# A block retention and two dense stages on one core: forming the scaled queries on GpSimd, and converting the second piece of the first weights inside the retention

## The chip, the cores and the metric

The kernel runs on one core of a Trainium2 chip. The metric is the device time of one execution in microseconds. Three runs of the kernel before gave 575.89, 576.50 and 577.19 us, a median of 576.5 us. The engines are called PE (matrix multiply), DVE (VectorE), ACT (ScalarE), POOL (GpSimd) and SP (the queue that issues most DMAs).

## The reference, cut to what matters

```python
for b in range(nb):                       # blocks along the sequence, per batch and head
    intra = (qb @ kb.T) * Dmask           # Dmask[i, j] = lam ** (i - j) for i >= j
    intra = intra @ vb
    inter = (qb * lam_pow) @ kv_state     # lam_pow[i] = lam ** (i + 1)
    out[block] = intra + inter
    kv_state = lam_block * kv_state + (kb * rev_pow).T @ vb
x = out as (1536, 512)                    # tokens by heads * head_dim
x = relu(x @ w_in) ** 2 @ w_out           # first dense stage, weights (512, 2048) and (2048, 512)
x = leaky(x @ w_in2) @ w_out2             # second dense stage, slope 0.01
```

Batch is 2, heads 8, sequence 768, head dimension 64. The weights arrive as 64-bit floats.

## The kernel before, in words

The retention is computed in chunks of 128 positions: 2 batches of 6 chunks give 12 units, called u0 to u11 here. A unit needs k, q and v (three loads of 256 KB, line 201). Of k and q PE makes transposes (L294), which ACT copies out of PSUM as kT and qT (L298). PE then forms raw scores (L311); DVE multiplies them by the table of powers and so makes Pm (mask, L316, two instructions of 128x512). Queries scaled by their powers, qS, are made by DVE out of the PSUM bank of the transposes (scale_q, L304); the first unit of a batch (u0, u6) needs none. The state of a unit is a product of v and decayed keys kd (PE L335; kd is made by POOL, L329), to which DVE adds the old state times a power (tmp by POOL at L342, sum st by DVE at L347, two instructions; L349 at the start of a batch). The output of a unit takes qS with the state of the unit before (L360) and Pm with v (L362). It leaves PSUM as a high part (ACT, L68, xhi) and a low part (DVE, L69, xlo), because each later product is made of three products of high and low parts.

PE's and SP's order in the retention is the program's own order. One pass of the loop at L391, called i, does: transposes and scaled queries of unit i+2, loads of k and q of unit i+4 and of v of unit i+2, at some i a fetch of a raw piece of weights, then state(i), output(i), mask(i+1), scores(i+2), and at some i a step of a conversion. DVE, ACT and POOL follow an order that a scheduler sets from the same code, and each engine runs its list in order. So a waiting instruction holds all that stands behind it.

A weight is fetched in pieces of 1 MB (fetch, L90, two buffers) and turned into a high and a low part by converting (L98): ACT takes the magnitude (L114), then DVE works in steps L115, L116, L118, L121, L122, L125, ACT casts the high part (L135), and DVE's last step L137 makes the low part. All are 128x1024. A call of convert (L153) issues one step. The first piece (first half of w_in's first slice) is fetched at i = 1 and converted in seven steps at i = 3 to 9; the second piece (w1h1, w1l1) is fetched at i = 9 and converted after the retention.

After the retention the dense stages follow on PE in a fixed order; all their products are at L503. The first group starts right behind the output of u11. What later groups of products read is formed on ACT and DVE at L468 to L499.

Of the kernel before, what the change touches and what calls it, by code (L numbers as in the profile page):

```python
# [14 lines left out]
ALU = mybir.AluOpType  # L15
# [4 lines left out]
def tile_retention_then_two_mlps(  # L20
# [12 lines left out]
    nc = tc.nc  # L33
# [56 lines left out]
    def fetch():  # L90
        if todo:
            key = todo.pop(0)
            r = raw.tile([P, 4 * CW], I64, tag="raw", name="raw")
            k = 4 if key[2] == 0 else 2
            dma(r.rearrange("p (k f) -> p k f", k=k), source(*key))
            fetched.append((key, r))
# [56 lines left out]
    def convert(pin=False):  # L153
        for piece in list(at_work):
            step = next(piece[1], False)
            if step is False:
                at_work.remove(piece)
            elif step is not None:
                if pin:
                    tc.keep_in_program_order(step)  # L160
                return
        if not fetched:
            return
        key = fetched[0][0]
        alike = sum(apart(k) == apart(key) for k, _ in at_work)
        if alike < (2 if not apart(key) or key[3] == 1 else 1):
            at_work.append((key, converting()))
            step = next(at_work[-1][1])
            if pin:
                tc.keep_in_program_order(step)  # L170
# [13 lines left out]
    def retention(ctx_att, att):  # L184
# [9 lines left out]
        nats, qT, kT, qS, Pm, raw_scores = {}, {}, {}, {}, {}, {}  # L194

        def load(i, which="kqv"):
            b, c = units[i]
            for name in which:
                t = nat[name].tile([P, H, D], F32, tag=name, name=name)
                src = {"q": q, "k": k, "v": v}[name]  # L200
                dma(t, src[b, :, c * C:(c + 1) * C, :].rearrange("h p d -> p h d"))
                nats[i, name] = t
# [4 lines left out]
        ve = nc.vector  # L207
# [59 lines left out]
        LR = att.tile([P, NP, C], F32, name="LR")  # L267
# [20 lines left out]
        def transposes(i, names="kq"):  # L288
            for name in names:
                dst = {"k": kT, "q": qT}[name]  # L290
                ps = bank().rearrange("p (a s) -> p a s", a=NP)
                src = nats[i, name]
                for p in range(NP):
                    nc.tensor.transpose(ps[:, p, :], src[:, 2 * p:2 * p + 2, :].rearrange("s h d -> s (h d)"), ident)  # L294
                if i == 0:
                    warm(3 if name == "k" else 4)
                dst[i] = tr.tile([P, NP, C], F32, tag=name, name=name + "T", bufs=2)
                nc.scalar.copy(dst[i], ps)  # L298
            return ps

        def scale_q(i, ps):
            if units[i][1]:
                qS[i] = tr.tile([P, NP, C], F32, tag="qS", name="qS")
                ve.tensor_tensor(out=qS[i], in0=ps, in1=LR, op=ALU.mult)  # L304

        def scores(i):
            raw_scores[i] = [bank().rearrange("p (a s) -> p a s", a=NP) for _ in range(2)]
            for p in range(NP):
                for par in range(2):
                    r = slice(par * D, (par + 1) * D)  # L310
                    nc.tensor.matmul(raw_scores[i][par][:, p, :], kT[i][r, p, :], qT[i][r, p, :], start=True, stop=True)  # L311

        def mask(i):
            Pm[i] = wk.tile([P, 2, NP, C], F32, tag="Pm", name="Pm")
            for par in range(2):
                ve.tensor_tensor(out=Pm[i][:, par], in0=raw_scores[i][par], in1=DT[:, par], op=ALU.mult)  # L316
# [34 lines left out]
        def output(n):  # L351
            b, c = units[n]
            vn = nats[n, "v"]
            ps = bank().rearrange("p (a s) -> p a s", a=NP)
            for p in range(NP):

                rows = [slice(par * D, (par + 1) * D) for par in range(2)]
                if c:
                    for r in rows:
                        nc.tensor.matmul(ps[r, p, :], st[c % 2][:, p, r], qS[n][:, p, :], start=True, stop=False)  # L360
                for par, r in enumerate(rows):
                    nc.tensor.matmul(ps[r, p, :], vn[:, 2 * p + par, :], Pm[n][:, par, p, :], start=c == 0, stop=True)  # L362
            t, o = divmod(b * S + c * C, TT)
            if xhi[t] is None:
                new_x(t)
            split(xhi[t][:, :, o:o + C], xlo[t][:, :, o:o + C], ps)
# [13 lines left out]
        column_of_powers()  # L380
        rows_of_powers()
        scale_q(1, q1)
        scores(1)
        state(0)
        mask(0)
        output(0)
        scale_q(2, transposes(2))
        state(1)
        mask(1)
        scores(2)  # L390
        for i in range(n_units):  # L391
            if i and i + 2 < n_units:
                scale_q(i + 2, transposes(i + 2))
            if i + 4 < n_units:
                load(i + 4, "kq")
            if i + 2 < n_units:
                load(i + 2, "v")
            if i in (1, 9):
                fetch()
            if i:  # L400
                if i > 1:
                    state(i)
                output(i)
                if i + 1 < n_units:
                    mask(i + 1)
                if i + 2 < n_units:
                    scores(i + 2)
            if 3 <= i <= 9:
                convert(pin=True)


    with ExitStack() as ctx_att:
        att = ctx_att.enter_context(tc.tile_pool(name="att", bufs=1))
        with tc.manual_schedule(engines={mybir.EngineType.SP, mybir.EngineType.PE}):
            retention(ctx_att, att)
# [368 lines left out]
```

## Time and profile before

| what | value |
|---|---|
| median of 3 runs | 576.5 us |
| the profiled execution | 576.09 us, of which the span of the trace is 574.3 us |
| PE busy | 564.1 us (98%), granted clock 1.00 throughout |
| DVE busy | 418.9 us (73%) |
| ACT busy | 304.4 us (53%) |
| POOL busy | 90.7 us (16%) |
| read and written in HBM | 55.05 and 30.42 MB |

The shares are averages over a retention (to about 64 us of the span) and the dense stages behind it. For the change the retention has to be read by itself: the times in the views are microseconds from the start of the span, and a row of a timeline gives start, duration, engine, line, operation, and in brackets how long the engine was idle before and what ended that.

### The profile page before, as it was taken

To read this page: it belongs to the slowest core of one execution; us is meant where nothing else is said; L and a number is where in the kernel's file an instruction comes from. 1 tells how busy PE (TensorE), PEld (TensorE's weight loads), DVE (VectorE), ACT (ScalarE), POOL (GpSimd) and SP (SyncE) were. 2 spreads that over 40 slices of the span, in tenths; PEclk is the share of its full clock that TensorE was granted. 3 is DMA by queue.
4 is the path that set the end of the run, shared out by engine and by line. 5 is a ranking of instruction groups with operands and counts; after the bars stand their busy time and mean duration, and the time that the engine had idled before them with its cause. 6 is when DMAs were issued, how large, how long until landed. Compare 5 with 4: busy or idle time off the path is not lost.

```text
span 574.3 us, 8060 instructions
## 1 busy us (share of the span) xinstructions
PE 564.1 (98%) x3075; PEld 470.4 (82%) x3075; DVE 418.9 (73%) x589; ACT 304.4 (53%) x477; POOL 90.7 (16%) x105
## 2 busy tenths in 40 slices
PE   7989999999999999999999999999999999999997
PEld 6879888888788888888888888888888888888886
DVE  3789999999927699498478999929883996217222
ACT  2344598547757587758447375453562376225110
POOL 3426000000044604343000000000213011310000
PEclk9999999999999999999999999999999999999999
DMA  8998434655498958999313215342529523661432
GB/s 173 244 201 188 155 121 135 233 184 190 163 156 138 155 175 183 211 258 227 128 36 95 80 33 218 130 164 74 105 53 246 110 33 42 76 89 56 164 111 91
DMA packets 79350, 80.75 MB, mean 141 GB/s; under 512 B 40264, under 2 KB 51792, under 8 KB 79312
## 3 DMA queue, kind: packets, MB, share of 16 engines
q1 hardware_dynamic: 61312, 62.15, 35.5%
q0 software_dynamic: 17472, 17.83, 22.9%
q8 instruction: 24, 0.39, 0.3%
q10 hardware_dynamic: 528, 0.26, 0.2%
q14 instruction: 14, 0.11, 0.1%
HBM read 55.05 MB, written 30.42 MB: 149 GB/s over the span
## 4 chain that ended last, share of the span: by engine, by line
PE 75%; DVE 16%; DMA 5%; issue 3%; ACT 1%; DVEq 0%; SPq 0%; ACTq 0%
PE ps L503 72%; DVE hb L118 2%; DVE rb L122 2%; DVE hb L125 2%; DMA v<-in_v 2%; DVE Pm L316 1%; DVE rb L121 1%; DVE hb L115 1%; DMA raw<-in_moe_w_in 1%; DVE xlo L69 1%; DMA raw<-in_moe_w_out 1%; DMA DTr<-tab 1%; DVE w2l L137 1%; PE ps L360 1%; DVE st L347 1%
## 5 line engine op out<-in xcount | busy, mean ns | idle before, releaser
L503 PE MATMUL ps<-xhi,w1h 128*128 128x512 f32 x288 | 112.2, 389 | 0.0
L503 PE MATMUL ps<-xhi,w1l 128*128 128x512 f32 x288 | 112.0, 389 | 0.0
L503 PE MATMUL ps<-xlo,w1h 128*128 128x512 f32 x288 | 112.0, 389 | 0.0
L616 POOL DMA_DIRECT2D spill<-f x48 | 47.9, 1215 | 349.9 <-ACT f L612 349.8
L612 ACT COPY f<-ps 128x512 f32<-128x512 f32 x84 | 48.7, 585 | 71.7 <-PE ps L503 71.2
L503 PEld LDWEIGHTS ps<-xhi,w1h 128*128 128x128 f32 x288 | 54.1, 188 | 11.4 <-issue 0.2
L503 PEld LDWEIGHTS ps<-xhi,w1l 128*128 128x128 f32 x288 | 54.1, 188 | 11.3
L503 PEld LDWEIGHTS ps<-xlo,w1h 128*128 128x128 f32 x288 | 54.1, 188 | 11.2
L474 DVE TENSOR_TENSOR g0l<-f,g0h 128x512 fp32r<-128x512 f32 x52 | 35.1, 687 | 32.5 <-ACT f L470 20.9
L503 PE MATMUL ps<-w2l,g0h 128*128 128x512 f32 (+1 forms) x132 | 50.5, 383 | 0.0
L503 PE MATMUL ps<-w2h,g0l 128*128 128x512 f32 (+1 forms) x132 | 50.5, 383 | 0.0
L503 PE MATMUL ps<-w2h,g0h 128*128 128x512 f32 (+1 forms) x132 | 50.5, 383 | 0.0
L137 DVE TENSOR_TENSOR w2l<-hb,w2h 128x1024 fp32r<-128x1024 f32 x16 | 19.5, 1222 | 39.8 <-ACT w2h L135 39.8
L114 ACT ACTIVATE hb<-raw 128x1024 f32<-128x1024 f32 x32 | 36.8, 1148 | 20.5 <-DVE w2l L137 7.5
L503 PE MATMUL ps<-g0h,w2h 128*128 128x512 f32 x104 | 40.5, 389 | 0.0
L503 PE MATMUL ps<-g0l,w2h 128*128 128x512 f32 x104 | 40.5, 389 | 0.0
L503 PE MATMUL ps<-g0h,w2l 128*128 128x512 f32 x104 | 40.5, 389 | 0.0
L122 DVE SCALAR_TENSOR_TENSOR rb<-raw,rb 128x1024 f32<-128x1024 uint32 x32 | 39.1, 1221 | 0.4
L125 DVE TENSOR_TENSOR hb<-hb,rb 128x1024 f32<-128x1024 f32 x32 | 39.1, 1221 | 0.4
L118 DVE SCALAR_TENSOR_TENSOR hb<-raw,hb 128x1024 uint32<-128x1024 uint32 x32 | 39.1, 1221 | 0.3
L567 DVE TENSOR_TENSOR f<-ps,f 128x512 f32<-128x512 f32 x40 | 26.2, 684 | 9.9 <-PE ps L503 9.9
L716 DVE TENSOR_TENSOR f<-ps,f 128x512 f32<-128x512 f32 (+1 forms) x25 | 16.7, 668 | 22.8 <-PE ps L503 22.8
(143 smaller groups left out, 1141.9 us busy)
## 6 DMA issues: line engine op xcount, KB each, us to landing
raw<-in_moe_w_in SPq DMA_DIRECT2D x16, 1024.0 KB, 5.6
raw<-in_moe_w_out SPq DMA_DIRECT2D x16, 1024.0 KB, 5.2
spill<-f POOLq DMA_DIRECT2D x48, 256.0 KB, 6.1
spill<-f SPq DMA_DIRECT2D x24, 256.0 KB, 2.8
f<-spill SPq DMA_DIRECT2D x24, 256.0 KB, 2.9
k<-in_k SPq DMA_DIRECT2D x12, 256.0 KB, 4.7
q<-in_q SPq DMA_DIRECT2D x12, 256.0 KB, 5.2
v<-in_v SPq DMA_DIRECT2D x12, 256.0 KB, 4.9
```

The lines of the kernel that those rows point to most:

```text
L69: nc.vector.tensor_tensor(out=lo, in0=src, in1=hi, op=ALU.subtract)
L114: nc.scalar.activation(hf, w_hi.bitcast(F32), AF.Abs)
L118: yield ve.scalar_tensor_tensor(out=hb, in0=w_hi, scalar=0xC0000000, in1=hb, op0=ALU.bitwise_and, op1=ALU.bitwise_or)
L122: yield ve.scalar_tensor_tensor(out=rf, in0=w_lo, scalar=2.0 ** -52, in1=rf, op0=ALU.mult, op1=ALU.mult)
L125: yield ve.tensor_tensor(out=hf, in0=hf, in1=rf, op=ALU.add)
L137: yield ve.tensor_tensor(out=lo, in0=hf, in1=hi, op=ALU.subtract)
L474: nc.vector.tensor_tensor(out=glo, in0=r, in1=ghi, op=ALU.subtract)
L503: nc.tensor.matmul(ps, a, b, start=start and n == 0, stop=stop and n == len(ops) - 1, skip_group_check=again)
L567: ve.tensor_tensor(out=out, in0=ps[h, where], in1=other, op=ALU.add)
L612: nc.scalar.copy(f, src)
L616: nc.gpsimd.dma_start(dst, f, accum_op=ALU.add)
L716: nc.vector.tensor_tensor(out=a, in0=ps, in1=a, op=ALU.add)
```

## The change

Three edits. scale_q is issued to POOL and reads ACT's copy qT in SBUF in place of the PSUM bank. The second piece is fetched at i = 6, not 9. The conversion takes one step at i = 3 to 5 and two at i = 6 to 10, thirteen in place of seven.

```diff
         def scale_q(i, ps):
             if units[i][1]:
                 qS[i] = tr.tile([P, NP, C], F32, tag="qS", name="qS")
-                ve.tensor_tensor(out=qS[i], in0=ps, in1=LR, op=ALU.mult)
+                nc.gpsimd.tensor_tensor(out=qS[i], in0=qT[i], in1=LR, op=ALU.mult)
...
-            if i in (1, 9):
+            if i in (1, 6):
                 fetch()
...
-            if 3 <= i <= 9:
+            for _ in range((3 <= i <= 10) + (6 <= i <= 10)):
                 convert(pin=True)
```

How the orders move. First DVE's list from the low part of u7's output to the state of u10, before (the two rows L347 are the state of u8, then of u9, then of u10; the masks are of u9, u10, u11):

```order
L69 TENSOR_TENSOR xlo_587<-ps,xhi_586 128x4x128
L316 TENSOR_TENSOR Pm<-ps,DTr 128x512 x2
L125 TENSOR_TENSOR hb<-hb,rb 128x1024
L304 TENSOR_TENSOR qS<-ps,LR 128x512
L347 TENSOR_TENSOR st_170<-ps,tmp 64x4x64 x2
L69 TENSOR_TENSOR xlo_842<-ps,xhi_841 128x4x128
L316 TENSOR_TENSOR Pm<-ps,DTr 128x512 x2
L137 TENSOR_TENSOR w1l_928<-hb,w1h_927 128x1024
L304 TENSOR_TENSOR qS<-ps,LR 128x512
L347 TENSOR_TENSOR st_168<-ps,tmp 64x4x64 x2
L69 TENSOR_TENSOR xlo_842<-ps,xhi_841 128x4x128
L316 TENSOR_TENSOR Pm<-ps,DTr 128x512 x2
L347 TENSOR_TENSOR st_170<-ps,tmp 64x4x64 x2
```

and the same stretch of DVE's list with the change:

```order
L69 TENSOR_TENSOR xlo_587<-ps,xhi_586 128x4x128
L316 TENSOR_TENSOR Pm<-ps,DTr 128x512 x2
L347 TENSOR_TENSOR st_170<-ps,tmp 64x4x64 x2
L115 TENSOR_SCALAR hb<-hb 128x1024
L116 TENSOR_SCALAR hb<-hb 128x1024
L69 TENSOR_TENSOR xlo_849<-ps,xhi_848 128x4x128
L316 TENSOR_TENSOR Pm<-ps,DTr 128x512 x2
L118 SCALAR_TENSOR_TENSOR hb<-raw,hb 128x1024
L347 TENSOR_TENSOR st_168<-ps,tmp 64x4x64 x2
L121 TENSOR_SCALAR rb<-hb 128x1024
L69 TENSOR_TENSOR xlo_849<-ps,xhi_848 128x4x128
L316 TENSOR_TENSOR Pm<-ps,DTr 128x512 x2
L347 TENSOR_TENSOR st_170<-ps,tmp 64x4x64 x2
```

Between the states of u8 and u10 one scaled query and one step (L137) were replaced by four steps (L115, L116, L118, L121) of the second piece; L125 and L137 of the first piece now stand ahead of this stretch, and L122 and L125 of the second piece behind it.

POOL's list over the last four units, with the change (before, the same without the rows L304):

```order
L329 TENSOR_TENSOR kd<-k,kdec 128x512
L304 TENSOR_TENSOR qS<-qT,LR 128x512
L342 TENSOR_TENSOR tmp<-st_168,LR 64x256 x2
L329 TENSOR_TENSOR kd<-k,kdec 128x512
L304 TENSOR_TENSOR qS<-qT,LR 128x512
L342 TENSOR_TENSOR tmp<-st_170,LR 64x256 x2
L304 TENSOR_TENSOR qS<-qT,LR 128x512
L342 TENSOR_TENSOR tmp<-st_168,LR 64x256 x2
```

A scaled query now stands between the decayed keys and the old state's product of each unit, ten of them in all.

SP's list at i = 6 to 9 (k and q are those of u11, the three v those of u9 to u11):

```order
 L65 DMA q<-in_q 128x8x64
 L65 DMA v<-in_v 128x8x64
+L65 DMA raw<-in_moe_w_in 128x4x256
 L65 DMA k<-in_k 128x8x64
 L65 DMA q<-in_q 128x8x64
 L65 DMA v<-in_v 128x8x64 x3
-L65 DMA raw<-in_moe_w_in 128x4x256
 L65 DMA raw<-in_moe_w_out 128x2x512 x3
```

The second piece has moved ahead of the last five loads of the retention. On ACT its L114 has moved to just behind qT of u10, ahead of xhi of u8 and of kT and qT of u11. PE's order is the same.

## Rows read from the trace of the kernel before

**Rows 1.** Busy time by stretch: length, PE, PEld, DVE, ACT, POOL, clock, DMA share, GB/s.
```profile
45.00:55.00 10.00, 10.00 (x162) 8.96 (x160) 9.63 (x17) 4.59 (x8) 7.38 (x9) 1.00 0.75 164
```

**Rows 2.** Timeline, PE: states of u2, u3, u8, u9; output of u11; first dense product.
```profile
23.93 0.69 PE L335 MATMUL ps<-v,kd 128*64 128x64 f32 x16
...
28.41 0.69 PE L335 MATMUL ps<-v,kd 128*64 128x64 f32 x16
...
51.22 0.69 PE L335 MATMUL ps<-v,kd 128*64 128x64 f32 x16
...
55.70 0.69 PE L335 MATMUL ps<-v,kd 128*64 128x64 f32 x16
...
61.42 0.76 PE L360 MATMUL ps<-qS,st 128*64 128x128 f32 x3
...
63.75 0.50 PE L503 MATMUL ps<-xhi,w1h 128*128 128x512 f32 x1
```

**Rows 3.** PE's transposes of u3, and the load of its k (issue, landing).
```profile
18.24 0.63 PE L294 MATMUL ps<-ident,k 128*128 128x128 f32 x4 [0.17 <-DVE qS L304]
...
L65 SPq DMA_DIRECT2D k<-in_k x1: 1192/1192/1192, 12.3 to 12.3; - x1
...
DMA to landing us min/median/max: 5.8/5.8/5.8
```

**Rows 4.** Timeline, PE: the only pause in the dense stages.
```profile
154.11 0.61 PE L503 MATMUL ps<-g1h,sw 128*128 128x512 f32 x2
155.11 0.50 PE L503 MATMUL ps<-g1l,sw 128*128 128x512 f32 x1 [0.38 <-DVE g1l L69]
```

**Rows 5.** Timeline, DVE, end of the retention; and ACT's cast of w1h.
```profile
53.02 0.68 DVE L304 TENSOR_TENSOR qS<-ps,LR 128x512 f32<-128x512 f32 x1
53.62 0.86 DVE L347 TENSOR_TENSOR st<-ps,tmp 64x256 f32<-64x256 f32 x2
54.70 0.69 DVE L69 TENSOR_TENSOR xlo<-ps,xhi 128x512 fp32r<-128x512 f32 x1 [0.21 <-ACT xhi L68]
55.31 1.28 DVE L316 TENSOR_TENSOR Pm<-ps,DTr 128x512 f32<-128x512 f32 x2
56.50 1.22 DVE L137 TENSOR_TENSOR w1l<-hb,w1h 128x1024 fp32r<-128x1024 f32 x1
...
58.24 0.87 DVE L347 TENSOR_TENSOR st<-ps,tmp 64x256 f32<-64x256 f32 x2
...
60.94 0.86 DVE L347 TENSOR_TENSOR st<-ps,tmp 64x256 f32<-64x256 f32 x2
61.84 0.70 DVE L115 TENSOR_SCALAR hb<-hb 128x1024 f32<-128x1024 f32 x1
...
53.14 1.05 ACT L135 CAST w1h<-hb 128x1024 fp32r<-128x1024 f32 x1 [1.12 <-DVE hb L125]
```

**Rows 6.** Timeline, DVE and POOL, where both work in SBUF.
```profile
35.78 1.27 DVE L116 TENSOR_SCALAR hb<-hb 128x1024 uint32<-128x1024 uint32 x1
...
47.45 1.22 DVE L122 SCALAR_TENSOR_TENSOR rb<-raw,rb 128x1024 f32<-128x1024 uint32 x1
...
35.46 1.04 POOL L329 TENSOR_TENSOR kd<-k,kdec 128x512 f32<-128x512 f32 x1 [0.75 <-PE ps L335]
...
47.57 2.00 POOL L329 TENSOR_TENSOR kd<-k,kdec 128x512 f32<-128x512 f32 x1 [1.02 <-issue]
...
58.72 1.31 POOL L342 TENSOR_TENSOR tmp<-st,LR 64x256 f32<-64x256 f32 x2 [3.31 <-DVE st L347]
```

**Rows 7.** Raw pieces in the first 70 us: landing; ACT's wait; chain; SP's k(u11).
```profile
raw<-in_moe_w_in SPq DMA_DIRECT2D x2, 1024.0 KB, 6.9
...
30.11 1.14 ACT L114 ACTIVATE hb<-raw 128x1024 f32<-128x1024 f32 x1 [3.12 <-DMA raw<-in_moe_w_in]
...
25.30 9.20 DMA v<-in_v
...
45.79 0.90 SPq L65 DMA_DIRECT2D k<-in_k  x1
```

## The prediction

> **What bounds the kernel now.** I read the busy time by stretch first, then PE's timeline, then DVE's and POOL's at the end of the retention, and last the loads. From 45 to 55 us PE is busy 10.00 of 10 us and DVE 9.63 [rows 1], so the averages do not say which of the two sets the pace. PE's own timeline does: the states of u2 and u3 start 4.48 us apart and those of u8 and u9 also 4.48 us apart [rows 2]. The first pair lies where DVE still has pauses, the second where it has nearly none, so 4.48 us is PE's own time for a unit, and DVE just keeps up. Before that, loads set the pace: the transposes of u3 start at 18.24, and the load of its k, issued at 12.3 and 5.8 us under way, lands at 18.1 [rows 3]; the row names DVE's qS as releaser only because it came last among several semaphores. The chain goes through a load of v that took 9.20 us from 25.30 [rows 7], so to 34.5 us nothing is won by a lighter DVE. Behind the retention PE runs without a pause but one, of 0.38 us at 155.11, where it waits for a low part made by DVE [rows 4].
>
> So time can change at three places: loads ahead of 34.5 us (not touched by the change: their issues keep their order), the end of the retention, and the pause at 155 us. What matters at the end of the retention is the state of u10. DVE adds it from 60.94 to 61.80 [rows 5]; the output of u11 is started on PE at 61.42 but needs it, and the first dense product follows at 63.75 [rows 2], 1.95 us behind the state's end. Whatever moves that state moves all of the dense part.
>
> **The change part by part.**
>
> *Ten scaled queries leave DVE.* Each is 0.60 us there (from 53.02 to the next start at 53.62 [rows 5]), 6.0 us in all. On POOL the nearest row is the decayed keys, the same shape and also two operands in SBUF: 1.04 us alone, 2.00 us when it starts inside a step of the conversion (47.57, inside L122 from 47.45 to 48.67) [rows 6]. I take these as both ends, 10.4 to 20 us on an engine that is busy 7.38 of 10 us from 45 to 55 us [rows 1], decayed keys and old states already among them. A scaled query is made two units ahead of its use, 9 us by the spacing above, so the product itself is hidden; who feels it are the old-state products queued behind it on POOL, and DVE's steps beside it.
>
> The Trainium skill (GPSIMD Engine Reference, Engine selection) says that elementwise work of two inputs belongs on VectorE and is about twice as slow on GpSimd. By that rule alone the ten cost some 12 us on POOL, an estimate from the page, and nothing in the sum as long as POOL keeps ahead.
>
> *Six more conversion steps enter DVE ahead of the dense part.* I go along DVE's list. Up to the state of u8, at 53.62 before: three scaled queries behind the output of u5 go (-1.80); L137 comes in (L137 and a scaled query take 56.50 to 58.24, so L137 is 1.14); it waits for ACT's cast of 1.05 us, of which the state's 0.9 us hides all but about 0.2 [rows 5]. So that state starts at 53.2 at best. What a two-operand step (L122, L125, L137) loses when POOL is already at work, no row shows: at least 0, at most POOL's remaining time, 1.04 us; the nearest row is L116, which lost 0.6 us there [rows 6], and only one or two steps meet POOL in flight, so I take 0.2 together: 53.4. A gain is excluded, since the steps have no faster form in the trace.
>
> From the state of u8 to that of u10 it was 7.32 us (53.62 to 60.94). Out go a pause of 0.21, the scaled query, 0.60, and L137, 1.14: 5.37 us are left. In come L118, priced as L137, 1.14, and L115, L116 and L121. These three have two prices: 0.6 to 0.7 us with POOL idle (61.84), and 1.2 to 1.27 us when POOL has started before them (35.78, the decayed keys since 35.46) [rows 5, 6]. L121 stands right behind the state of u9, and POOL's old-state product starts just when the first half of that state is there (58.72, where the state began at 58.24) [rows 5, 6], so they meet. L115 stands behind the state of u8 in the same way, and with the scaled queries in its list POOL goes from one product to the next in that stretch, so L116 meets one as well. I take 1.2 us for each, 3.6 us: 5.37 + 1.14 + 3.6 = 10.1 us. The state of u10 then starts at 53.4 + 10.1 = 63.5, which is **2.55 us later** than 60.94. With the low price it would be 8.3 us behind 53.2, at 61.5: 0.5 us later. Those are the ends.
>
> The Trainium skill (GPSIMD Engine Reference, Key points) says that GpSimd shares its SBUF interfaces with VectorE and contends with its two-port modes and with instructions of two SBUF inputs. The trace agrees: 1.27 against 0.70 us for the one, 2.00 against 1.04 us for the other [rows 5, 6].
>
> PE's delay at the outputs of u9 and u10 (the state of u9 ends about a microsecond late) lies inside these 2.55 us. The second piece's L122 and L125 stand behind the state of u10 and cost the retention nothing.
>
> *The earlier fetch.* The piece takes the place at which SP issued k of u11, 45.79, and by the median of its like (6.9 us [rows 7]) lands at 52.7. ACT's L114, 1.14 us, then ends at 53.9 and L115, due at 54.3, is not held: 0. Queued behind L114 on ACT are the copies kT and qT of u11, which PE needs for its scores only after the state of u9 and its output: 0. Queued behind the piece on SP are k and q of u11 and v of u9 to u11. The v behind the first piece took 9.20 us [rows 7]; the state of u9, at 55.70, needs the v that stands behind the second. PE may wait there for up to 2 us, but DVE reaches the state of u9 only at about 59, so this hides behind the 2.55 us. Without that cover it would cost what it waits.
>
> *After the retention.* DVE has some 6 us less to do by 155 us, less what contention took, so the pause there goes: the third product before it began at about 154.34, the next was due 0.23 later, at 154.57, and came at 155.11 [rows 4]: **-0.55 us**. The dense part is otherwise PE's own time and PE's order is the same.
>
> Sum: +2.55 - 0.55 = +2.0 us on the profiled execution of 576.09 us, whose span is 574.3 us: 578.1 us. That execution lies 0.41 us below the median of the runs shown, 576.5; I keep 578.1, which is 0.28% over the median. Changes of under 0.2%, 1.15 us, can hardly be told from none here.
>
> **The rivals.**
>
> *POOL out of the way (not slower).* If L115, L116 and L121 find POOL idle, the state of u10 is 0.5 us late and the pause of 0.55 us is gone: 576.0 us. For it: L115 at 61.84 ran in 0.70 us. Against it: POOL's list has one product more in each unit. It decides if all three run under 0.8 us; one of them slow gives 576.6. If POOL alone set the state (two kd and three qS at 2.00 us and three tmp at 1.31 us from 48.4, where a scaled query lets it begin), its last tmp would end at 62.3 and the state of u10 about 1 us late: 576.5 us, of this case too.
>
> *The raw piece late (slower still).* If it takes as long as the worst load of the stretch, 9.20 us, it lands at 55.0, L114 ends at 56.1, and DVE stands 1.8 us at L115 with the masks of u10 and u11 and both states behind it; half of that is likelier, 579.0, and the whole 579.9. For it: L114 waited 3.12 us for the first piece [rows 7]. Against it: the two of this stretch took 6.9 us at the median.
>
> *Both waits go (faster).* If DVE gains more before u8 than it loses after, PE waits neither for the state of u10 (0.4 us, 61.42 to 61.80) nor at 155 us: 575.1 us. That would need the four steps in the room of one step and one scaled query.
>
> That the change does not do what it says: only in so far as L122, L125 and L137 of the second piece still fall behind the retention's last state.
>
> **How the numbers follow.** Forecast (577.4 to 578.8) 0.48; POOL out of the way (575.6 to 577.2) 0.27; raw piece late (578.8 to 580) 0.15; both waits go (574.9 to 575.6) 0.10. Slower by over 1.15 us, above 577.65: 0.41 of the first and 0.14 of the third, 0.55. Faster, below 575.35: 0.06 of the last and 0.02 of the second, 0.08. The rest, 0.37, is the same. The range 575.8 to 579.6 leaves out the last case and the far end of the third. The likeliest case's own range is 577.4 to 578.8.
>
> **What would show it.** Right: the first dense product near 66.3; L115, L116 and L121 between the states of u8 and u10 at 1.2 us or more; PE's longest new wait for the state of u10; no pause at 155 us. Wrong: these steps at 0.7 us, or the first dense product at or before 64.3; L115 preceded by a wait for L114 and the raw piece; PE held at the state of u9 by a load of v longer than DVE needs.

## The result and the profile after

The changed kernel takes **583.88 us** (median of 6 runs, 580.72 to 586.98); the kernel before, on the same chip, 576.68 us (6 runs, 575.80 to 577.35). The ratio is 1.0123, 95% interval 1.0094 to 1.0152: slower by 7.2 us, where 578.1 us and a range to 579.6 us were forecast. The profiled execution took 583.70 us, its span is 581.9 us (574.3 before).

The page of the changed kernel, busy time in us, share of the span and number of instructions of each engine:

```profile
PE 567.3 (97%) x3075; PEld 472.1 (81%) x3075; DVE 416.5 (72%) x579; ACT 304.5 (52%) x477; POOL 104.5 (18%) x115
```

The totals tell little: DVE lost 2.4 us of work, POOL gained 13.8, and PE is busy for 3.2 us more with the same products. Where the time went is read from PE's own timeline of the changed kernel (start, duration, engine, line, operation; in brackets the idle time before and what ended it):

```profile
67.20 0.50 PE L503 MATMUL ps<-xhi,w1h 128*128 128x512 f32 x1
...
157.32 0.39 PE L503 MATMUL ps<-g1l,sw 128*128 128x512 f32 x1
157.55 0.39 PE L503 MATMUL ps<-g1h,sw 128*128 128x512 f32 x1
159.90 0.49 PE L503 MATMUL ps<-g1h,sw 128*128 128x512 f32 x1 [1.97 <-ACT g1h L68]
160.65 0.50 PE L503 MATMUL ps<-g1l,sw 128*128 128x512 f32 x1 [0.25 <-DVE g1l L69]
...
162.82 0.63 PE L503 MATMUL ps<-g1h,sw 128*128 128x512 f32 x1
163.24 0.63 PE L503 MATMUL ps<-g0h,w2h 128*128 128x512 f32 x1
163.67 0.63 PE L503 MATMUL ps<-g0l,w2h 128*128 128x512 f32 x1
```

The first dense product starts at 67.20, not at 63.75 [rows 2]: **3.45 us are lost at the end of the retention**. From there to the start of the last product it is 510.55 us (577.75), before 506.78 us (570.53): **3.77 us are lost in the dense stages**. The sum is 7.22 us; the spans differ by 7.56 us, and the rest, 0.34 us, lies behind the start of the last product. The second loss lies in one place. Products that start 0.23 us apart stop at 157.55, and two come 2.12 and 0.52 us late, where before one came 0.55 us late (0.38 us of it idle [rows 4]); then, from 162.39, they start 0.43 us apart, about 1.4 us in all, before the old spacing is back at 165.3. The windows of the changed kernel (length, then busy time of PE, PEld, DVE, ACT, POOL, granted clock, DMA share, GB/s) name this:

```profile
158.00:160.00 2.00, 0.10 (x1) 0.10 (x1) 1.97 (x6) 0.77 (x2) 0.00 (x0) 1.00 0.00 0
...
162.00:164.00 2.00, 2.00 (x6) 1.62 (x5) 1.93 (x4) 0.87 (x3) 0.00 (x0) 0.50 0.50 187
```

PE works 0.10 of 2 us from 158 to 160; after the pause the granted clock is 0.50, the lower of the two levels (1.2 GHz). These products belong to the first of two stages in which PE multiplies pairs of token groups with sums of weights (tile sw); I call them the first and the second pair.

**First loss.** DVE's timeline at the end of the retention, with the change; it answers to [rows 5]:

```profile
43.99 0.87 DVE L349 COPY st<-ps 64x256 f32<-64x256 f32 x2
...
47.95 1.65 DVE L125 TENSOR_TENSOR hb<-hb,rb 128x1024 f32<-128x1024 f32 x1
...
50.73 2.10 DVE L137 TENSOR_TENSOR w1l<-hb,w1h 128x1024 fp32r<-128x1024 f32 x1 [0.33 <-ACT w1h L135]
...
54.66 0.87 DVE L347 TENSOR_TENSOR st<-ps,tmp 64x256 f32<-64x256 f32 x2
55.56 1.34 DVE L115 TENSOR_SCALAR hb<-hb 128x1024 f32<-128x1024 f32 x1
56.93 1.00 DVE L116 TENSOR_SCALAR hb<-hb 128x1024 uint32<-128x1024 uint32 x1
...
59.77 1.22 DVE L118 SCALAR_TENSOR_TENSOR hb<-raw,hb 128x1024 uint32<-128x1024 uint32 x1
...
61.80 0.76 DVE L121 TENSOR_SCALAR rb<-hb 128x1024 uint32<-128x1024 uint32 x1
...
64.39 0.87 DVE L347 TENSOR_TENSOR st<-ps,tmp 64x256 f32<-64x256 f32 x2
```

The state of u10 starts at 64.39, 3.45 us later, and the first dense product 2.81 us behind it, as before. The clearest measure is the time from the copy that begins the second batch (L349, state of u6) to the state of u10, since it leaves out by how much that copy itself moved: 16.19 us before (from this row to 60.94 [rows 5]), **20.40 us** now.

```profile
44.75 0.86 DVE L349 COPY st<-ps 64x256 f32<-64x256 f32 x2
```

**Second loss.** What the late pair waits for is a high part by ACT, behind a sum by DVE, behind this on ACT and DVE:

```profile
141.84 1.13 ACT L114 ACTIVATE hb<-raw 128x1024 f32<-128x1024 f32 x1 [3.66 <-DMA raw<-in_moe_w_out]
...
143.00 0.70 DVE L115 TENSOR_SCALAR hb<-hb 128x1024 f32<-128x1024 f32 x1 [3.26 <-ACT hb L114]
```

A raw piece was issued at 133.46 and landed 8.36 us later, and DVE stood for 3.26 us, 15 us ahead of the pair. In the kernel before the same piece was issued at 131.43, ACT waited 0.83 us for it, and DVE did not stand. What those 3.26 us mean is seen when DVE's busy time is laid beside that of before (20 us windows, the kernel before and then the changed one):

```profile
126.00:146.00 20.00, 20.00 (x90) 16.56 (x89) 19.70 (x24) 14.15 (x22) 0.00 (x0) 1.00 0.59 191
146.00:166.00 20.00, 19.62 (x87) 15.93 (x86) 14.85 (x24) 13.62 (x25) 5.38 (x6) 1.00 0.61 125
```

```profile
126.00:146.00 20.00, 20.00 (x90) 16.53 (x90) 16.45 (x20) 11.07 (x17) 0.00 (x0) 1.00 0.54 170
146.00:166.00 20.00, 17.78 (x70) 14.01 (x69) 18.45 (x28) 13.56 (x25) 0.83 (x1) 0.91 0.40 132
```

Ahead of the pair DVE is full (19.70 of 20 us). The 3.25 us that it loses from 126 to 146 are made up from 146 to 166, when PE needs its results. (From 129.45 to 149.45, the same stretch behind the first dense product, DVE of the changed kernel is busy 16.48 us, so the first loss does not explain the difference.)

### The profile page after: what moved, and what is told of

The parts are those of the page before. It is cut to its first block, busy times and chain, and to the rows that moved or that the text cites. A ratio compares the mean times of both kernels' runs of the same rounds, so it can differ in the third digit from the quotient of the medians.

```text
span 581.9 us, 8058 instructions
## 1 busy us (share of the span) xinstructions
PE 567.3 (97%) x3075; PEld 472.1 (81%) x3075; DVE 416.5 (72%) x579; ACT 304.5 (52%) x477; POOL 104.5 (18%) x115
## 4 chain that ended last, share of the span: by engine, by line
PE 73%; DVE 14%; DMA 7%; issue 2%; ACT 2%; SPq 1%; POOL 0%; DVEq 0%; POOLq 0%; ACTq 0%
PE ps L503 72%; DMA raw<-in_moe_w_in 3%; DMA raw<-in_moe_w_out 3%; DVE rb L122 2%; DVE hb L125 1%; DVE hb L118 1%; DVE hb L115 1%; DMA k<-in_k 1%; DVE Pm L316 1%; SPq L65 1%; DVE rb L121 1%; DVE xlo L69 1%; ACT hb L114 1%; DVE hb L116 0%; DVE sw L442 0%
## 5 line engine op out<-in xcount | busy, mean ns | idle before, releaser
L503 PE MATMUL ps<-xhi,w1h 128*128 128x512 f32 x288 | 112.1, 389 | 0.0
L503 PE MATMUL ps<-xhi,w1l 128*128 128x512 f32 x288 | 112.0, 389 | 0.0
L503 PE MATMUL ps<-xlo,w1h 128*128 128x512 f32 x288 | 112.0, 389 | 0.0
L503 PEld LDWEIGHTS ps<-xhi,w1h 128*128 128x128 f32 x288 | 54.1, 188 | 11.4 <-issue 0.2
L503 PEld LDWEIGHTS ps<-xhi,w1l 128*128 128x128 f32 x288 | 54.1, 188 | 11.2
L503 PEld LDWEIGHTS ps<-xlo,w1h 128*128 128x128 f32 x288 | 54.1, 188 | 11.2
L503 PE MATMUL ps<-w2l,g0h 128*128 128x512 f32 (+1 forms) x132 | 50.5, 383 | 0.0
L503 PE MATMUL ps<-w2h,g0l 128*128 128x512 f32 (+1 forms) x132 | 50.5, 383 | 0.0
L503 PE MATMUL ps<-w2h,g0h 128*128 128x512 f32 (+1 forms) x132 | 50.5, 383 | 0.0
L114 ACT ACTIVATE hb<-raw 128x1024 f32<-128x1024 f32 x32 | 36.8, 1151 | 25.9 <-DMA raw<-in_moe_w_out 9.0
L137 DVE TENSOR_TENSOR w2l<-hb,w2h 128x1024 fp32r<-128x1024 f32 x16 | 19.5, 1222 | 39.8 <-ACT w2h L135 39.8
L503 PE MATMUL ps<-g0h,w2h 128*128 128x512 f32 x104 | 40.9, 394 | 0.0
L503 PE MATMUL ps<-g0l,w2h 128*128 128x512 f32 x104 | 40.9, 393 | 0.0
L503 PE MATMUL ps<-g0h,w2l 128*128 128x512 f32 x104 | 40.7, 391 | 0.0
L125 DVE TENSOR_TENSOR hb<-hb,rb 128x1024 f32<-128x1024 f32 x32 | 39.5, 1234 | 0.4
L122 DVE SCALAR_TENSOR_TENSOR rb<-raw,rb 128x1024 f32<-128x1024 uint32 x32 | 39.1, 1221 | 0.5
L118 DVE SCALAR_TENSOR_TENSOR hb<-raw,hb 128x1024 uint32<-128x1024 uint32 x32 | 39.1, 1221 | 0.4
```

The costliest lines, as they stand in the source:

```text
L114: nc.scalar.activation(hf, w_hi.bitcast(F32), AF.Abs)
L118: yield ve.scalar_tensor_tensor(out=hb, in0=w_hi, scalar=0xC0000000, in1=hb, op0=ALU.bitwise_and, op1=ALU.bitwise_or)
L122: yield ve.scalar_tensor_tensor(out=rf, in0=w_lo, scalar=2.0 ** -52, in1=rf, op0=ALU.mult, op1=ALU.mult)
L125: yield ve.tensor_tensor(out=hf, in0=hf, in1=rf, op=ALU.add)
L137: yield ve.tensor_tensor(out=lo, in0=hf, in1=hi, op=ALU.subtract)
L503: nc.tensor.matmul(ps, a, b, start=start and n == 0, stop=stop and n == len(ops) - 1, skip_group_check=again)
```

## The experiments

Each run's kernel was timed beside runs of the kernel before. The last three columns are of one profiled execution: state of u6 to state of u10 on DVE; start of the first dense product; from there to the start of the last.

| run | ratio to before (95%) | u6 to u10 | first | first to last |
|---|---|---|---|---|
| before | 1 | 16.19 | 63.75 | 506.78 |
| the change | 1.0123 (1.0094 to 1.0152) | 20.40 | 67.20 | 510.55 |
| e1 | 0.9990 (0.9976 to 1.0003) | 16.45 | 62.26 | 506.74 |
| e2 | 1.0127 (1.0103 to 1.0151) | 20.29 | 69.16 | 511.51 |
| e3 | 1.0046 (1.0026 to 1.0066) | 16.18 | 62.77 | 510.84 |
| e6 | 1.0075 (1.0046 to 1.0104) | 20.40 | 66.95 | 510.91 |
| e7 | 1.0009 (1.0000 to 1.0019) | 16.45 | 63.24 | 507.11 |
| e8 | 1.0132 (1.0118 to 1.0146) | 20.40 | 67.85 | 510.65 |
| e9 | 1.0035 (1.0022 to 1.0047) | 16.18 | 63.46 | 508.79 |
| e10 | 1.0031 (1.0011 to 1.0051) | 17.20 | 63.71 | 507.90 |
| e11 | 1.0047 (1.0028 to 1.0065) | 18.78 | 64.91 | 509.17 |
| e12 | 1.0133 (1.0119 to 1.0147) | 20.40 | 67.11 | 511.13 |
| e13 | 1.0002 (0.9992 to 1.0013) | 16.45 | 63.28 | 506.97 |
| e14 | 1.0051 (1.0035 to 1.0068) | 20.39 | 67.01 | 506.09 |

### Which of the three edits

**e1**, the kernel before with the queries alone:

```diff
-                ve.tensor_tensor(out=qS[i], in0=ps, in1=LR, op=ALU.mult)
+                nc.gpsimd.tensor_tensor(out=qS[i], in0=qT[i], in1=LR, op=ALU.mult)
```

> Scaled queries on GpSimd alone; fetch at i = 9 and seven steps as before. Theory A (the end of the retention is paced by DVE's list, and the added steps are what it cannot hold): DVE's list loses 0.6 us a unit, so the first dense product stands at 63.2 to 64.0 us (before 63.75) although L125 and L137 may take 1.6 to 2.1 us beside GpSimd; no pause of PE at 155 us; 575.5 to 576.8 us. Rival (the queries on GpSimd are the loss by themselves, through late old-state products and slowed steps): first dense product at 65 us or later, 578 us or more.

Measured: 575.73 us beside 576.79, and in a second set (e13, below) 576.21 beside 576.23. No loss, and no gain that can be told. DVE has 0.6 us less in each unit and yet u6 to u10 is not shorter: PE sets that pace, as the prediction had it, and L122 and L125 took 1.55 and 1.56 us beside GpSimd in place of 1.22.

**e2**, the other two edits without it:

```diff
-            if i in (1, 9):
+            if i in (1, 6):
...
-            if 3 <= i <= 9:
+            for _ in range((3 <= i <= 10) + (6 <= i <= 10)):
```

> Early fetch and thirteen steps, scaled queries left on DVE. Theory A (too many steps for DVE, whoever forms the queries): DVE's list from the state of u8 to that of u10 is 9.0 to 10.7 us, first dense product at 66.5 to 68.5 us. Rival (GpSimd beside the steps is the loss): all steps at their short durations (1.22 and 0.70 us) and first dense product below 65.3 us. In either case the pause at 155 to 160 us stays if it comes from ACT's order, since the list of ACT there is that of the changed kernel: 580 to 586 us by A, below 578 us by the rival without the pause.

Measured: 584.58 us beside 576.79; both losses are here. u6 to u10 takes 20.29 us though DVE makes the queries itself: what DVE saved by the queries in the changed kernel, GpSimd's work beside its steps took back. Its first dense product comes 4.22 us behind the state of u10, not 2.81: PE stood 2.63 us for that state, and from 66 to 69 us, in the output of u11, the granted clock was 0.54. Behind the retention e2 has the changed kernel's lists to the last instruction. The second loss (4.73 us from first to last product) is not smaller than there, but on PE's timeline of e2 it stands ahead of the second pair:

```profile
222.89 0.39 PE L503 MATMUL ps<-g1h,sw 128*128 128x512 f32 x1
225.11 0.50 PE L503 MATMUL ps<-g1h,sw 128*128 128x512 f32 x1 [1.83 <-ACT g1h L68]
226.20 0.50 PE L503 MATMUL ps<-g1l,sw 128*128 128x512 f32 x1 [0.58 <-DVE g1l L69]
```

**e3**, the earlier fetch alone, with the second piece's L114 held to its place in the program on ACT:

```diff
-        nc.scalar.activation(hf, w_hi.bitcast(F32), AF.Abs)
+        mag = nc.scalar.activation(hf, w_hi.bitcast(F32), AF.Abs)
+        if key == (0, 0, 0, 1):
+            tc.keep_in_program_order(mag)
...
-            if i in (1, 9):
+            if i in (1, 6):
```

> The second piece is fetched at i = 6, nothing else in the retention changed (its conversion starts behind the retention; the order of ACT and DVE in the dense part shifts with it). Theory A: the loads behind the piece hold PE for at most 1 us at the transposes of u11 and the state of u9 (in the changed kernel 0.50 and 0.16 us), and this shows at the first dense product only as far as DVE is not later still: 63.8 to 64.8 us. Rival (late loads are the main loss): 66 us or later.

Measured: 579.92 us beside 576.79. The end of the retention is that of before (16.18 us), and still 4.06 us are lost in the dense stages, at the first pair. That spoke for the fetch as the cause of the second loss. But this kernel's lists behind the retention are not those of before either, so the run does not part the fetch from the lists; e7 does.

**e7**, the changed kernel with single steps; from the first dense group on its lists are those of the kernel before:

```diff
-            for _ in range((3 <= i <= 10) + (6 <= i <= 10)):
+            if 3 <= i <= 10:
```

> The changed kernel with one step a unit instead of two at the end of the retention (units 3 to 10); queries on GpSimd and the early fetch stay. Behind the retention its lists on ScalarE, VectorE and SyncE are those of the kernel before. Theory A (both losses hang on the doubled steps: 4.2 us at the end of the retention by VectorE, and the second loss only because the doubled steps lead to other lists behind the retention, in which a raw piece lands late): no second loss, VectorE from the copy of the first state of the second half to its last state 16 to 17 us (20.40 in the changed kernel), time 575 to 577 us. Rival B (the early fetch itself brings the second loss, since it moves all later transfers, whatever the lists): a pause of 2 us ahead of a pair of products and half clock behind it, 579.5 to 581 us.

Measured: 576.70 us beside 576.50, 16.45 us from u6 to u10; 0.56 us are lost at the first pair (0.67 before) and 0.43 us at the second (none before). So with the queries on GpSimd **and** the earlier fetch in place both losses are gone: the first is the doubled steps, 3.96 us between this run's first dense product (63.24) and the changed kernel's, and the second hangs on the lists: e3 pays it with other lists and not one doubled step, e7 has the lists of before and is 0.33 us over before from first to last product. The earlier fetch by itself costs nothing that can be told.

### How the losses grow with the steps

**e10** and **e11**, the changed kernel with two steps a unit only from i = 9, and only from i = 8:

```diff
-            for _ in range((3 <= i <= 10) + (6 <= i <= 10)):
+            for _ in range((3 <= i <= 10) + (9 <= i <= 10)):      # e10; in e11 (8 <= i <= 10)
```

> The changed kernel with two steps a unit only for units 9 and 10. Between the copy of the first state of the second half and the last state VectorE gets one step more than with single steps (L115, 0.7 us alone), where the changed kernel gets four more. In the run with single steps VectorE was busy some 4.0 of each 4.49 us between states, so it has about 0.5 us a unit to spare. Theory A (the end of the retention costs what exceeds that spare time): 16.4 to 16.8 us from the copy to the last state (16.45 with single steps, 20.40 in the changed kernel). The second loss is one of all or nothing: the lists behind the retention are neither those of the kernel before nor those of the changed one, so it is there with 2 to 4 us (578.5 to 581 us) if a piece lands late in a stage where VectorE is full, and then VectorE's wait for L114 ahead of L115 is over 5 us in the stretch from 66 to 230 us (3.0 before, 3.4 with single steps, 7.0 in the changed kernel). Rival B (both losses grow in proportion to the additional steps, a quarter of them here): 577.5 to 579 us, 17.4 us from copy to last state.

> The changed kernel with two steps a unit only for units 8 to 10: two steps more ahead of the last state than with single steps (L115 and L116, 1.4 us alone). SyncE's list is that of the changed kernel. Theory A: 16.8 to 17.8 us from the copy to the last state, and the second loss as in the changed kernel (some 4 us, VectorE's wait for L114 ahead of L115 over 5 us): 580 to 582.5 us. Rival B (both losses in proportion to the additional steps, half of them here): 18.4 us from copy to last state, 579 to 580.5 us with a pause of 1 us ahead of the pair and no half clock.

Measured: 578.12 and 579.26 us beside 576.25. From u6 to u10 they take 0.75 and 2.33 us more than e7, the changed kernel 3.95. So my spare time of 0.5 us was not there (in the unit into which the step falls, DVE of e7 stands for 0.18 us), and one additional step (L115, 0.87 us) already came out almost whole. The rows of e11 show why two more cost over 2 us:

```profile
53.51 2.10 DVE L137 TENSOR_TENSOR w1l<-hb,w1h 128x1024 fp32r<-128x1024 f32 x1 [0.32 <-ACT w1h L135]
...
57.45 1.24 DVE L115 TENSOR_SCALAR hb<-hb 128x1024 f32<-128x1024 f32 x1
```

The first piece's last step moves into GpSimd's work and takes 0.88 us more than alone, and the second piece's first step 0.55 us more. The second loss isn't all or nothing either: 0.8 us in e10, at the second pair alone, and 2.1 us in e11, at both, all without a fall of the clock in the dense stages (first to last product, against e7). In these kernels it goes with one number of the waits, DVE's wait for L114 ahead of L115 from 66 to 230 us:

| | before | e7 | e10 | e11 | the change |
|---|---|---|---|---|---|
| DVE's wait for L114, us in all | 3.0 | 3.4 | 5.4 | 6.6 | 7.0 |
| the longest of these | 1.2 | 1.5 | 3.0 | 2.9 | 3.3 |
| first to last product, over before | 0 | 0.33 | 1.12 | 2.39 | 3.77 |

The sum of these waits does not fix the loss, though: e3 has 6.0 us of them and loses 4.06, e14 (below) has 4.4 us and loses nothing. It matters where they lie.

### What the second loss is made of

**e6**, the changed kernel with the late piece's L114 held to its place in the program, behind the first pair's activations:

```diff
-        nc.scalar.activation(hf, w_hi.bitcast(F32), AF.Abs)
+        mag = nc.scalar.activation(hf, w_hi.bitcast(F32), AF.Abs)
+        if key == (0, 2, 1, 1):
+            tc.keep_in_program_order(mag)
```

> The changed kernel, but the one L114 that holds ACT at 138 to 142 us (second half of w_out's third slice) is pinned behind the work of ACT that the program has ahead of it. Theory B (this wait for a raw piece in ACT's queue delays the high parts for the pair of products and is the cause of PE's pause at 157.6 us and of the half clock behind it): first dense product still at 67.2 us, pause of PE under 0.6 us, clock 1.00 throughout, 578.5 to 580.5 us. Rival (the pause comes from PE's late start, or from DVE's load): pause of 1.5 us or more, 582 us or more.

Measured: 580.60 us beside 576.79, runs from 579.34 to 583.90. The pause at the first pair is gone, so that late piece did cause it. But in the profiled execution (583.77 us) a pause of the same size stands ahead of the second pair, with the clock at 0.57 behind it (PE's timeline of e6, where L505 is L503 of the other kernels, and then a window of e6):

```profile
222.28 0.50 PE L505 MATMUL ps<-g1h,sw 128*128 128x512 f32 x1 [2.02 <-ACT g1h L68]
223.37 0.50 PE L505 MATMUL ps<-g1l,sw 128*128 128x512 f32 x1 [0.59 <-DVE g1l L69]
```

```profile
224.00:228.00 4.00, 4.00 (x12) 3.13 (x11) 4.00 (x7) 2.91 (x6) 0.86 (x1) 0.57 0.85 278
```

Here it is a piece of w_in, issued at 202.26, for which ACT waits 4.9 us at 212.58.

**e8**, the changed kernel with one addition of the late piece, ahead of the first pair, moved to GpSimd:

```diff
-        yield ve.tensor_tensor(out=hf, in0=hf, in1=rf, op=ALU.add)
+        yield (nc.gpsimd if key in ((0, 2, 1, 1),) else ve).tensor_tensor(out=hf, in0=hf, in1=rf, op=ALU.add)
```

> The changed kernel with a single addition moved from VectorE to GpSimd: L125 of the piece whose transfer landed late (1.22 us on VectorE at 154.90, ahead of the high and low parts that the pair of products waits for). The lists of ScalarE and SyncE are those of the changed kernel, and the piece still lands late. Theory A (VectorE has no slack in this stage, so its 3.3 us of idle time come out as the pause): VectorE gets 1.1 to 1.2 us back, the pause ahead of the pair falls from 2.0 to about 0.8 us and the half clock behind it may go, 580 to 582.8 us. Rival B (the pause is set by ScalarE's order, in which the conversion's first operation stands ahead of the activations): no change, 583.3 to 584.5 us.

Measured: 583.95 us beside 576.50. PE's pause at the first pair is 2.21 us, the granted clock stays at 1.00 behind it, and 1.0 us is lost at the second pair. The help was eaten up at once:

```profile
152.72 2.89 DVE L488 TENSOR_TENSOR g1l<-f,g1h 128x512 fp32r<-128x512 f32 x1
...
152.37 2.69 POOL L125 TENSOR_TENSOR hb<-hb,rb 128x1024 f32<-128x1024 f32 x1 [88.69 <-DVE rb L122]
```

DVE's L488, 0.69 us everywhere else, took 2.89 us beside GpSimd's addition: 2.2 us lost for 1.22 saved. Beside the trace of the changed kernel this still speaks against rival B. In e8 ACT began L114 73.6 us behind the first dense product (141.47), 1.0 us earlier than in the changed kernel (74.6), and the pause was no shorter; DVE was given the same 1.0 us and lost it to L488.

**e9**, the kernel before with DVE held for four operations ahead of L115 of that piece:

```diff
+        if key == (0, 2, 1, 1):
+            for _ in range(4):
+                ve.tensor_scalar(out=rb, in0=hb, scalar1=0xFF800000, scalar2=None, op0=ALU.bitwise_and)
         yield ve.tensor_scalar(out=hf, in0=hf, scalar1=2.0 ** -15, scalar2=122368.0, op0=ALU.max, op1=ALU.min)
```

> The kernel before with four additional operations of some 0.65 us on VectorE (2.6 us in all, written into a tile that is written again before it is read) ahead of L115 of the same piece; the lists of SyncE and GpSimd are those of before, nothing lands later, and on ScalarE only the casts behind the held VectorE change places with a neighbour. Theory A (no slack on VectorE in this stage): the pause ahead of the pair, 0.55 us in the kernel before, grows to 2 to 3 us, with half clock behind it for some 2 us, 578.8 to 581.5 us. Rival B (VectorE could have been held; what costs is the late transfer holding ScalarE): within 0.5 us of the kernel before.

Measured: 578.08 us beside 576.50: 2.0 us more from first to last product, but not where I expected them. At the first pair 0.94 us is lost, 0.67 before, since the scheduler moved other steps of DVE behind it; 1.7 us came out at the second pair, at 217.4. I had expected that nothing lands later, and that did not hold: ACT waits 3.40 us for the piece of w_in ahead of the second pair, 1.49 before, and DVE stands with it (before, then e9, whose L118 is L115 of the other kernels):

```profile
207.85 0.69 DVE L115 TENSOR_SCALAR hb<-hb 128x1024 f32<-128x1024 f32 x1 [0.97 <-ACT hb L114]
```

```profile
209.73 0.69 DVE L118 TENSOR_SCALAR hb<-hb 128x1024 f32<-128x1024 f32 x1 [2.87 <-ACT hb L114]
```

So e9 does not show that the held time was carried from one pair to the next: a late piece alone can be these 1.7 us (the table under e14). The amount held (2.6 us) came out in part, at the wrong place for theory A, and not at all as rival B had it.

**e12**, the changed kernel with two steps of the late piece left out (the exponent bits and the sign of these weights):

```diff
-        nc.scalar.activation(hf, w_hi.bitcast(F32), AF.Abs)
+        mag = nc.scalar.activation(hf, w_hi.bitcast(F32), AF.Abs)
...
+        if key == (0, 2, 1, 1):
+            yield mag
+            yield mag
+        else:
             yield ve.tensor_scalar(out=hb, in0=hb, scalar1=3, scalar2=0x3FFFFFFF,
...
             yield ve.scalar_tensor_tensor(out=hb, in0=w_hi, scalar=0xC0000000, in1=hb,
```

> The changed kernel without L116 and L118 of the one piece that lands late (1.9 us of VectorE's work behind its L114, left out with the part of these weights that they form); ScalarE's list has that L114 at the same place, SyncE's and GpSimd's lists are those of the changed kernel. Theory A (VectorE's lost time is what the pair of products waits for): with 1.9 us less to do behind the late landing the pause ahead of the pair falls from 2.0 us to under 0.5 us and the half clock behind it goes, so the time falls by 1.9 to 3.8 us, to 580 to 582 us. Rival B (the late L114 on ScalarE holds the activations ahead of the pair, whatever VectorE has to do): the pause stays at 1.7 us or more, 583 to 585 us.

Measured: 583.93 us beside 576.23. The pause at the first pair went, as theory A said, and the time did not: 2.08 and 0.86 us now stand ahead of the second pair, with the lower clock behind them, and first to last product is 4.35 us over before. As in e6 and e2 the piece of w_in is what is late there. What removed the pause at the first pair is not parted: there was 1.9 us less of work, but also a piece for which ACT waited 1.81 us, not 3.66, and DVE 1.40 us, not 3.26. In e2 nothing is left out, DVE waits 1.57 us for this piece, and at the first pair no more is lost than before. One kind of cause, a late piece, stands behind both pairs, and which pair pays differs: in the changed kernel itself, where PE has already lost 4 us at the first pair, the piece of w_in is in time (ACT waits 1.66 us for it).

**e14**, e6 without the four last accumulating transfers by GpSimd in this stage (DMAs that add to what stands at their destination; their part of the sum is left out); ACT, DVE and SP have e6's lists to the last instruction:

```diff
             for dst, src in ((p67, p1), (kept(p, 0, 1), p1), (kept(p, 0, 1), p6), (kept(p, 1, 0), p67),
                              (kept(p, 1, 1), p67)):
+                if s == 1 and src is p67:
+                    continue
                 nc.gpsimd.dma_start(dst, src, accum_op=ALU.add, max_dma_last_dim=TT)
```

> The changed kernel with L114 of the late piece pinned (the earlier experiment, whose pause ahead of the first pair was gone and came 2.2 us long ahead of the second pair at 220 us instead, after a piece for which ScalarE waited 4.9 us), now without the four last accumulating transfers that GpSimd issues in this stage (L686, the sum of partial products added to two of its places; the part of the result that they add is left out). The lists of ScalarE, VectorE and SyncE are the same to the last instruction. Theory C (the piece lands late because it shares the transfer engines with GpSimd's accumulating transfers, and VectorE's time lost by it is the pause): ScalarE's wait for the piece falls from 4.9 us to 2 us or less (1.5 in the kernel before), the pause ahead of the second pair to under 0.6 us, the half clock behind it goes, 576.5 to 578.3 us. Rival D (the lists of the changed kernel leave the conversion behind by some 4 us whatever the transfers do, and that comes out once, ahead of one pair or another): the pause stays or moves to a later place, 580 to 581.5 us.

Measured: 579.27 us beside 576.19, all runs between 578.86 and 579.62. The windows from 208 to 212 and from 220 to 224 us, first of e6, then of e14:

```profile
208.00:212.00 4.00, 4.00 (x20) 3.30 (x19) 1.30 (x2) 0.00 (x0) 0.00 (x0) 1.00 1.07 328
...
220.00:224.00 4.00, 1.40 (x6) 0.72 (x5) 4.00 (x6) 3.05 (x7) 0.00 (x0) 1.00 0.11 8
```

```profile
208.00:212.00 4.00, 4.00 (x20) 3.30 (x19) 4.00 (x7) 3.62 (x6) 0.00 (x0) 1.00 0.74 266
...
220.00:224.00 4.00, 4.00 (x19) 3.30 (x18) 4.00 (x7) 3.12 (x6) 1.24 (x1) 1.00 0.94 324
```

With the four transfers away the raw piece is there when ACT comes to it (L114 starts 5.4 us behind its issue, 10.3 us in e6), DVE works 4.00 of 4 us where it had 1.30, PE has no pause, and first to last product is 506.09 us. What remains, 3.1 us, is the first loss. So at the second pair the chain is shown from end to end in these two executions: a piece that is under way beside GpSimd's transfers lands late, ACT's L114 and with it DVE stand, and DVE has no room to make it up before the pair. The accumulating transfers and the three stores behind them in GpSimd's queue are not parted, since without the four these stores too are issued 4.5 to 8.1 us earlier.

The other traces agree. In order of DVE's wait for this piece ahead of L115 (lost: by how much the starts of the products at the second pair lie further apart than undisturbed, in us):

| | e14 | before | e1 | the change | e13 | e3 | e7 | e8 | e9 | e11 | e10 | e2 | e12 | e6 |
|---|---|---|---|---|---|---|---|---|---|---|---|---|---|---|
| DVE's wait | 0 | 0.97 | 1.01 | 1.17 | 1.33 | 1.35 | 1.49 | 1.97 | 2.87 | 2.90 | 3.01 | 4.21 | 4.33 | 4.44 |
| lost at the second pair | 0 | 0 | 0 | 0 | 0.2 | 0.1 | 0.4 | 1.0 | 1.7 | 1.7 | 1.8 | 4.6 | 4.7 | 4.8 |

Beyond some 1.2 us, each microsecond for which DVE stands there is about one lost at the pair; the last three have some 1.6 us more by the lower clock.

The median fell by only 1.3 us against e6 (0.7 us, when each is set against the runs of before beside it), and the intervals of the two ratios overlap: e6's own runs go from 579.34, the level of e14, to 583.90, so it seems to pay this loss in some executions and not in others.

**e13**, e1 a second time.

> The kernel before with the queries scaled on GpSimd alone, a second time, to tell whether it beats the kernel before: 0.999 the first time (0.9976 to 1.0003). From first to last product of the dense part it took 506.74 us, before 506.78 us, so all it can gain lies in the retention: 0 to 1.5 us, 575.2 to 576.7 us beside 576.5 us.

Measured: 1.0002 (0.9992 to 1.0013). No version tried here beats the kernel before: its dense part has under 1 us of pauses in 506.78 us, and at the end of the retention PE sets the pace.

**What stays open.** Why the piece issued at 133.46 took 8.36 us in the changed kernel and some 5.4 us before wasn't tried: the same kind of stores stand beside it in both, one more in flight here. And that the changed lists bring GpSimd's last accumulations about 2 us later against PE (the last two of them begin 128.9 us behind the first dense product before, 129.3 in e7, 131.0 in e6) is read from traces, not tested. The lists of ACT, DVE and SP in the changed kernel, e2 and e12 differ from those of before only to 164 us; at the second pair it is the times that differ, not the order.

## Why the prediction was wrong, by its steps

- **What bounds the kernel**: right. e1 takes 6 us of work from DVE and gains nothing measurable, and its states of u7 and u8 are still 4.49 us apart; the end of the retention starts the dense part 2.81 us behind the state of u10, in every run but e2 (4.22 us, at the lower clock).
- **Term 1, the six steps, +2.55 us: right in mechanism, too small.** Measured +3.45. The part between the states of u8 and u10 came out as forecast, 9.73 us against 10.1 (the three one-input steps at 1.34, 1.00 and 0.76, not 1.2 each). The error is ahead of it: the state of u8 was due at 53.4 and started at 54.66. The step that failed is the 0.2 us put down for two-operand steps that meet GpSimd in flight. L125 and L137 took 1.65 and 2.10 us, where alone they take 1.22: 1.31 us for two steps. I had named the bound myself (GpSimd's remaining time, 1.04 us each) and then chosen near its other end.
- **Term 2, the fetch, 0**: right as far as the retention goes (L114 at 52.34, waiting 0.20 us), and e7 shows it for the whole kernel.
- **Term 3, the pause at 155 us, -0.55 us: wrong in sign**, and the larger error, 4.3 us. I reasoned from DVE's amount of work ("some 6 us less to do by 155 us") and from PE's unchanged order. What came was 3.77 us more. An engine that is busy for 19.70 of 20 us ahead of a deadline is hurt by when its inputs arrive, not only by how much it has to do. The steps brought forward gave ACT, DVE and SP other lists for the next 100 us, and with those lists raw pieces landed late. I compared the lists only up to the first dense product.
- **The rivals**: "the raw piece late" was the right mechanism at the wrong piece. I priced it for the second piece inside the retention (at most 1.8 us) and not for the pieces behind it, where DVE is just as full and the clock falls on top. "POOL out of the way" fell by its own sign, since it asked for all three one-input steps under 0.8 us and L115 took 1.34 and L116 1.00; and "both waits go" with both losses.

## What to carry to other kernels

Moving work ahead in a kernel whose lists a scheduler makes can change the lists of several engines behind it (here for 100 us, in e7 not): compare all of them, to the end, and look for each deadline (here the two pairs) at whether the engine ahead of it has time to spare. Where it has none, a late transfer far ahead of the deadline is paid there (3.3 us on DVE, 2.6 us on PE 15 us later, and more by the clock), and taking it away at one deadline may only move it to the next, so follow the time from the first product to the last and not a single pause. To find which edit carries a loss, take the edits out one at a time from the changed kernel, and choose the variant whose other lists are those of before.

## What the runs showed of the hardware

- DVE's price beside GpSimd is larger than the rows of before let see: steps of two SBUF operands 1.22 us alone, 1.55 to 1.65 and 2.10 us when GpSimd's elementwise work was in flight; L488 of half that size 0.69 us, and 2.89 us beside an addition of 2.69 us on GpSimd. GpSimd's scaled query took 1.27 us at its median and up to 2.31, the decayed keys of the same shape 1.04. In e8 GpSimd's addition runs from 152.37 to 155.06 and L488, begun at 152.72, ends at 155.61, about its own time behind it; L137 of the changed kernel in the same way ends 1.1 us behind a scaled query (from 50.47, 1.27 us). The Trainium skill (SBUF — State Buffer, Who interferes with whom) says that only the port pair that VectorE and GpSimd share contends, as an exclusive lock, that a VectorE instruction with two SBUF inputs meets a GpSimd instruction that reads SBUF there, and that issue order decides who blocks; these rows agree.
- The granted clock fell to its lower level behind two products that came late by 2.12 and 0.52 us (the change) and by 1.5 to 2.2 and 0.9 to 1.6 us (e2, e3, e6, e12), which cost a further 1.4 to 1.6 us. It stayed at 1.00 around 0.7 to 0.8 and 0.5 to 0.9 us (e9, e10, e11), but also around 2.37 and 0.50 us in e8, so here the length of the pauses alone does not tell whether it falls.
- Times spread by 6.3 us over six runs of the changed kernel, by 4.6 us over six of e6, and by 0.8 us over six of e14, which lacks only four transfers. That a transfer close to a deadline makes the spread fits this and is not shown, since one execution of each was traced.
